# Stores moved to GpSimd, sums of x on engines, and an earlier first fetch in a fused attention and two-MLP kernel

## The chip, the cores and the metric

The kernel runs on one core of a Trainium2 chip. The metric is the device time of one execution in microseconds (us); of several timed runs the median counts. The profile is of one further execution.

## The reference

Sliding-window attention with sink columns feeds two MLPs in a row, all in float32.

```python
# q, k, v: [2, 8, 768, 64]; window 128, 4 sink columns
a = softmax(where(is_sink | in_window, q @ k.T / 8, -1e9))
x = (a @ v).transpose(0, 2, 1, 3).reshape(1536, 512)
# first MLP: 512 -> 2048 -> 512
h = x @ w_in
g = where(h >= 1, h, where(h <= -1, 0, (h + 1) ** 2 / 4))
x = g @ w_out
# second MLP, its own weights
h = x @ w_in
out = (h * clip(h + 3, 0, 6) / 6) @ w_out
```

The weights come in as float64.

## The kernel before

x is held transposed, [512, 1536], as 4 blocks of 128 rows (KC) and 3 chunks of 512 tokens (NCH). The 2048 features are 16 chunks of 128 (FC), taken in 8 pairs. For float32 accuracy every operand of TensorE is split into a high and a low part; a product is three matmuls (high x high, high x low, low x high) for each 128 rows.

**Weights.** `load_w` fetches a pair of one weight (1 MB, 64-bit words) into one of two raw buffers; `narrow` turns the words into float32 with integer operations on VectorE and ScalarE, `split` makes the parts (`high` on either engine, `low` on VectorE). w_out's parts are also stored to DRAM (`wo_d`), since they are used twice. `turn_weights` does this for the next pair and asks for a further load three ticks later; `issued` and `taken` count both. From the third pair on (PLAIN is 2), `combine` also makes four sums of blocks of w_in, for a form of block multiplication that needs fewer products (`paired`, with the matching sums of x from `combine_x`). The sums are made in the raw buffer.

**Two stages for each MLP (m is 0 or 1).** First stage: for each chunk of features, h for the three token chunks. Token chunk 0 goes on at once: `activate`, then `y_group` accumulates its output in four PSUM banks. Token chunks 1 and 2 are kept in one of four buffers (`hq`) and stored to DRAM (`spill` to `h_d`). In `paired` a part of them is added in DRAM by an accumulating DMA (`add_c`). Second stage: `fetch` brings h back, `activate` and `y_group` run for chunks 1 and 2, and `load_wo` brings the split w_out back, into one of three buffers.

**Order.** TensorE's and SyncE's instructions keep the order of the program; the other engines' order is chosen by a scheduler with a timeline of its own, and is then fixed. Each queue runs in order. All DMAs but the accumulating ones are issued by SyncE (SP). `tick` and `defer` place work some groups later in the program.

In the code: the end of the first stage, its fetches and loads, and `start` are at the end of the main loop; L627 is the matmul of `product`, L779 that of `y_group`; L137 and L144 are `high` and `low`; L603 to L608 are `activate`; L677 is the subtraction in `combine_x`, L673 and L674 its DMAs; L715 and L710 evict products in `paired`; L719 is `add_c`; L189 to L199 are `narrow`; L642 is `spill`, L648 `fetch`, L276 `load_wo`, L233 the store of w_out's parts.

Of the kernel before, what the change touches and what calls it, by code (L numbers as in the profile page):

```python
# [71 lines left out]
def sink_attention_moe_moe_kernel(  # L72
# [75 lines left out]
    def x_tiles(m, c):  # L148
        if (m, c) not in xparts:
            xparts[m, c] = tuple(  # L150
                x_p.tile([P, KC, N], F32R, tag=f"x{part}{c}", name=f"x{part}{m}_{c}") for part in "hl"
            )
        return xparts[m, c]
# [47 lines left out]
    def take(m, which, p, half=None):  # L201

        fs = slice(0, 2) if half is None else slice(half, half + 1)
        n = DM * (fs.stop - fs.start)
        last = half is None or half == 1
        if (m, which, p) not in wtile:
            if which == "i":
                w = wi_p.tile([P, 2, 2, DM], F32R, tag="wi", name=f"wi{m}")
                for e in range(2):
                    wi[m, 2 * p + e] = tuple(w[:, x, e, :].rearrange("p (k f) -> p k f", f=P) for x in range(2))  # L210
            else:
                w = wo_tile(m, p)
            t = raw[m, which, p]
            if wide:
                t32 = raw_p.tile([P, 2, DM], F32, tag=f"w{which}32", name="w32", bufs=2 if which == "i" else 1)
            else:
                t32 = t
            wtile[m, which, p] = (w, t, t32)
        w, t, t32 = wtile[m, which, p]
        if last:  # L220
            raw.pop((m, which, p))
            wtile.pop((m, which, p))
        if which == "i":
            hi, lo = w[:, 0, fs, :], w[:, 1, fs, :]
        else:
            hi, lo = w[:, fs, 0, :], w[:, fs, 1, :]

        def split():
            high(hi, t32[:, fs], n)
            defer(lambda: low(lo, t32[:, fs], hi, n))  # L230
            if last and which == "o":
                defer(
                    lambda: nc.sync.dma_start(out=wo_d[m][p], in_=f32(w.rearrange("p t a f -> p (t a f)"))), 4  # L233
                )
            if last and which == "i" and p >= PLAIN:
                defer(lambda: combine(m, p, t, t32))
# [9 lines left out]
    def combine(m, p, t, t32):  # L246
# [47 lines left out]
    def build_fast_attention(at_p):  # L294
# [178 lines left out]
        def mix(j):  # L473
# [30 lines left out]
            xh, xl = x_tiles(0, GROUPS[gi][0])  # L504
            cs = slice(col0[gi], col0[gi] + n)
            high(xh[:, hp, cs], ps, n, True)
            low(xl[:, hp, cs], ps, xh[:, hp, cs], n)
# [79 lines left out]
    def load_x1():  # L587
        for c in range(NCH):
            xh, xl = x_tiles(0, c)
            for kc in range(KC):  # L590
                t = g_p.tile([P, N], F32, tag="r", name="xraw")
                nc.sync.dma_start(out=t, in_=x1_d[0][kc * P:(kc + 1) * P, c * N:(c + 1) * N])
                high(xh[:, kc, :], t, N)
                low(xl[:, kc, :], t, xh[:, kc, :], N)

    def activate(m, fc, c, h, g, psum):

        r = g_p.tile([P, N], F32, tag="r", name="r")
        gh = g_p.tile([P, N], F32R, tag="gh", name="gh", bufs=3)
        gl = g_p.tile([P, N], F32R, tag="gl", name="gl", bufs=3)  # L600
        with tc.high_priority(200):
            if m == 0:
                nc.scalar.activation(out=r, in_=h, func=AF.Relu, scale=0.5, bias=half)  # L603
                nc.scalar.activation(out=r, in_=r, func=AF.Square)  # L604
                nc.vector.scalar_tensor_tensor(out=g, in0=r, scalar=1.0, in1=h, op0=ALU.min, op1=ALU.max)
# [3 lines left out]
        bal.add("act", (2 - m) * (260 + N / 1.2))  # L609
        bal.add("dve", 150 + N / 0.96)  # L610
# [12 lines left out]
    def product(ps, w, x, start=True):  # L623
        (hi, lo), (xh, xl) = w, x
        ops = [(a, b, kc) for kc in range(hi.shape[1]) for a, b in ((hi, xh), (hi, xl), (lo, xh))]
        for i, (a, b, kc) in enumerate(ops):
            nc.tensor.matmul(  # L627
                ps, a[:, kc, :], b[:, kc, :], start=start and i == 0, stop=i == len(ops) - 1,
# [21 lines left out]
    def h_group(m, fc, c):  # L650
        ps = bank_h()
        product(ps, wi[m, fc], x_tiles(m, c))
        if c == 0:
            activate(m, fc, c, ps, ps, True)
# [6 lines left out]
    xt = {}  # L661

    def combine_x(m):

        t = st_p[0].tile([P, 2, 4, HK, N], F32R, tag="xt", name=f"xt{m}", bufs=1)
        xt[m] = [tuple(t[:, x, i] for x in range(2)) for i in range(4)]
# [3 lines left out]
        for i, (c, k) in enumerate(blocks):  # L670
            xh, xl = x_tiles(m, c)
            ks = slice(k * HK, (k + 1) * HK)
            nc.sync.dma_start(out=u[i], in_=f32(xh[:, ks, :]))  # L673
            nc.gpsimd.dma_start(out=u[i], in_=f32(xl[:, ks, :]), accum_op=ALU.add)  # L674
# [18 lines left out]
    def paired(m, p):  # L693
# [11 lines left out]
        def part(x, ks):  # L705
            return tuple(v[:, ks, :] for v in x)
# [18 lines left out]
        product(a, part(wi[m, f0], k0), part(xb, k0))  # L725
# [4 lines left out]
        product(a, part(wi[m, f0], k1), part(xb, k1), start=False)  # L730
        put(hf0[:, 0], a)
        tick()
# [18 lines left out]
        plus(hf1[:, 0], b)  # L751
        tick()
        product(c, s4, part(xc, k1), start=False)
# [5 lines left out]
    def y_group(m, fc, c):  # L759
# [11 lines left out]
        if last:  # L771
            if m == 0:
                xh, xl = x_tiles(1, c)
            else:
                o = x_p.tile([P, KC, N], F32, tag=f"xh{c}", name=f"o{c}")
        for dm in range(KC):
# [4 lines left out]
            if last:  # L781
                with tc.high_priority(400):
                    if m == 0:
                        high(xh[:, dm, :], ys[dm], N, True)
                        low(xl[:, dm, :], ys[dm], xh[:, dm, :], N)
                    elif dm % 2 == 0:
                        nc.scalar.activation(out=o[:, dm, :], in_=ys[dm], func=AF.Copy)
# [24 lines left out]
    with tc.manual_schedule(engines={mybir.EngineType.PE, mybir.EngineType.SP}):  # L812
        nc.vector.memset(half, 0.5)
        make_identity(nc, ident)
        if fast:
            with tc.tile_pool(name="at", bufs=2) as at_p:
                build_fast_attention(at_p)
                halves = {112: ("i", 0), 100: ("i", 1), 88: ("o", 0), 76: ("o", 1)}
                for n, step in enumerate(steps):
# [27 lines left out]
        issued[0] = taken[0] = 2  # L847
        st_p.append(ctx.enter_context(tc.tile_pool(name="st", bufs=2)))

        for m in range(2):  # L850
            for p in range(NP):
# [3 lines left out]
                for fc in (2 * p, 2 * p + 1):  # L855
# [27 lines left out]
            order = [(m, fc, c) for fc in range(FC) for c in (1, 2)]  # L883

            def start(k):
                _, fc, c = order[k]
                t = held[m, fc][:, c - 1]
                activate(m, fc, c, t, t, False)

            start(0)  # L890
            start(1)
            y_group(m, FC - 1, 0)
            tick()
            for n, (_, fc, c) in enumerate(order):
# [4 lines left out]
                if n + 2 < len(order):  # L899
                    start(n + 2)  # L900
# [50 lines left out]
```

## Time and profile before

| | |
|---|---|
| median of 3 runs | 689.57 us (688.48 to 691.66) |
| the profiled execution | 683.08 us, span 681.3 us |
| mean granted clock of TensorE | 0.970 |
| TensorE matmuls (PE) | 620.5 us busy, 91% of the span, 2,880 instructions |
| weight loads (PEld) | 482.6 us, 71% |
| VectorE (DVE) | 437.7 us, 64% |
| ScalarE (ACT) | 368.9 us, 54% |
| GpSimd (POOL) | 87.0 us, 13%, nearly all in the attention stage |
| DMA | 129.6 MB, 190 GB/s on average |

Attention lies in the first 111 us, the first stages at 111 to 289 and 395 to 572, the second ones at 298 to 395 and 582 to 677. Busy shares are averages over stages that wait for different things, and matmuls overlap in the pipeline with modelled ends, so that the number of matmuls in a stretch says more than the busy time.

### The profile page before, as it was taken

How to read it: one execution, taken by the hardware profiler on the slowest of the kernel's cores; microseconds unless marked ns; L12 is line 12 of the kernel's file. 1: busy time of each engine (PE TensorE's matmuls, PEld its weight loads, DVE VectorE, ACT ScalarE, POOL GpSimd, SP SyncE). 2: the span in 40 equal slices, each digit the busy share in tenths (PEclk: the TensorE clock that was granted, in tenths of full speed). 3: DMA queues.
4: the chain of work that ended last, by engine and by line, in shares of the span. 5: the costliest groups of instructions: out<-in, count | busy, mean ns of one | idle time of the engine just before them, and what ended most of it. 6: DMA issues, size and time to landing. Idle time of an engine off the chain costs nothing.

```text
span 681.3 us, 8173 instructions
## 1 busy us (share of the span) xinstructions
PE 620.5 (91%) x2880; PEld 482.6 (71%) x2880; DVE 437.7 (64%) x835; ACT 368.9 (54%) x671; POOL 87.0 (13%) x112
## 2 busy tenths in 40 slices
PE   7999899979999998959999997999999996899897
PEld 4666566858777776748767785888778884787676
DVE  5778886399787887344433846888877614545553
ACT  6878776377565656376564736465654514431211
POOL 6766751100000000000000020000000000000000
PEclk9999898979999999969999998999999998899999
DMA  6456213956687775485435587466687535944423
GB/s 209 131 159 190 61 63 134 285 200 246 248 254 241 214 242 166 106 291 211 158 124 199 203 248 220 160 229 207 208 250 235 189 93 176 342 166 157 167 105 125
DMA packets 42297, 129.60 MB, mean 190 GB/s; under 512 B 3600, under 2 KB 13328, under 8 KB 38160
## 3 DMA queue, kind: packets, MB, share of 16 engines
q1 hardware_dynamic: 37840, 118.58, 49.2%
q0 software_dynamic: 4416, 10.49, 9.2%
q8 instruction: 23, 0.38, 0.2%
q14 instruction: 18, 0.15, 0.1%
HBM read 77.68 MB, written 42.99 MB: 177 GB/s over the span
## 4 chain that ended last, share of the span: by engine, by line
DMA 32%; PE 30%; DVE 22%; ACT 11%; issue 3%; SPq 1%; POOL 0%; ACTq 0%; DVEq 0%; POOLq 0%
PE ps_y L779 13%; DMA hq<-h_d 12%; PE ps_h L627 11%; DMA raw0i<-moe_w_in_dram 5%; DMA raw1i<-moe_w_in_dram 3%; ACT p L425 3%; DVE w L194 3%; DVE w L199 3%; DVE gl L144 3%; DMA raw0o<-moe_w_out_dram 3%; ACT r L603 2%; DMA raw1o<-moe_w_out_dram 2%; DMA x<-xl 2%; DMA h_d<-hq 2%; ACT w L189 2%
## 5 line engine op out<-in xcount | busy, mean ns | idle before, releaser
L779 PE MATMUL ps_y<-gh,wo 128*128 128x512 f32 x768 | 251.1, 399 | 22.3 <-DMA wo<-wo_d 18.1
L779 PEld LDWEIGHTS ps_y<-gh,wo 128*128 128x128 f32 x768 | 148.1, 193 | 58.4 <-ACT r L604 9.4
L779 PE MATMUL ps_y<-gl,wo 128*128 128x512 f32 x384 | 154.9, 403 | 12.7 <-DVE gl L144 12.7
L627 PE MATMUL ps_h<-xh,wi 128*128 128x512 f32 x480 | 156.2, 391 | 2.0 <-ACT p L710 1.9
L627 PEld LDWEIGHTS ps_h<-xh,wi 128*128 128x128 f32 x480 | 90.5, 189 | 22.8 <-ACT p L710 3.1
L779 PEld LDWEIGHTS ps_y<-gl,wo 128*128 128x128 f32 x384 | 74.1, 193 | 33.7 <-DVE gl L144 18.7
L627 PE MATMUL ps_h<-xl,wi 128*128 128x512 f32 x240 | 93.7, 390 | 0.0
L144 DVE TENSOR_TENSOR gl<-hq,gh 128x512 fp32r<-128x512 f32 x64 | 44.0, 688 | 48.5 <-ACT gh L137 47.7
L416 POOL TENSOR_SCALAR p<-p,sm 128x260 f32<-128x260 f32 (+2 forms) x72 | 62.6, 885 | 34.0 <-DVE psk L407 18.7
L192 DVE TENSOR_SCALAR w<-w 128x1024 f32<-128x1024 f32 (+1 forms) x34 | 22.7, 668 | 58.2 <-ACT w L189 58.0
L425 ACT ACTIVATE p<-p,nm 128x260 f32<-128x260 f32 (+2 forms) x96 | 46.2, 483 | 16.2 <-DVE nm L392 16.0
L719 POOL DMA_DIRECT2D h_d<-ct x12 | 13.0, 1086 | 323.5 <-DMA h_d<-hq 76.6
L627 PE MATMUL ps_h<-xt,st 128*128 128x512 f32 x216 | 53.2, 390 | 0.7 <-DVE hq L715 0.7
L627 PEld LDWEIGHTS ps_h<-xl,wi 128*128 128x128 f32 x240 | 45.2, 188 | 9.2
L607 ACT ACTIVATE r<-hq,half 128x512 f32<-128x512 f32 x32 | 21.6, 715 | 49.1 <-DMA hq<-h_d 48.8
L627 PEld LDWEIGHTS ps_h<-xt,st 128*128 128x128 f32 x216 | 40.5, 188 | 9.5 <-DVE hq L715 1.1
L608 DVE SCALAR_TENSOR_TENSOR hq<-r,hq 128x512 f32<-128x512 f32 x32 | 21.5, 689 | 34.5 <-ACT r L607 34.5
L603 ACT ACTIVATE r<-hq,half 128x512 f32<-128x512 f32 x32 | 21.5, 714 | 35.6 <-DMA hq<-h_d 35.6
L392 DVE CUSTOM_DVE_ANT_0 p<-ps_s,mask 128x260 f32<-128x260 f32 (+2 forms) x96 | 34.4, 396 | 6.5 <-POOL mask L311 3.8
L379 PE MATMUL ps_s<-kraw,qraw 64*128 64x260 f32 (+2 forms) x192 | 32.4, 431 | 6.1 <-DMA kraw<-k_dram 4.4
L715 DVE TENSOR_TENSOR hq<-ps_h,p 128x512 f32<-128x512 f32 x36 | 24.6, 684 | 18.1 <-PE ps_h L627 18.1
L137 ACT ACTIVATE gh<-hq 128x512 fp32r<-128x512 f32 x43 | 26.5, 620 | 10.1 <-PE ps_y L779 9.4
(104 smaller groups left out, 862.7 us busy)
## 6 DMA issues: line engine op xcount, KB each, us to landing
h_d<-hq SPq DMA_DIRECT2D x32, 512.0 KB, 4.5
wo_d<-wo SPq DMA_DIRECT2D x16, 1024.0 KB, 9.3
hq<-h_d SPq DMA_DIRECT2D x32, 512.0 KB, 4.3
wo<-wo_d SPq DMA_DIRECT2D x16, 1024.0 KB, 6.8
raw1i<-moe_w_in_dram SPq DMA_DIRECT2D x8, 1024.0 KB, 7.0
raw1o<-moe_w_out_dram SPq DMA_DIRECT2D x8, 1024.0 KB, 9.1
raw0i<-moe_w_in_dram SPq DMA_DIRECT2D x7, 1024.0 KB, 6.1
raw0o<-moe_w_out_dram SPq DMA_DIRECT2D x7, 1024.0 KB, 9.9
```

The lines of the kernel that those rows point to most:

```text
L137: nc.scalar.activation(out=dst, in_=src, func=AF.Copy)
L144: nc.vector.tensor_tensor(out=dst, in0=src, in1=f32(hi), op=ALU.subtract)
L192: nc.vector.tensor_scalar(out=f32(c), in0=f32(c), scalar1=F64_LOW, scalar2=F64_HIGH, op0=ALU.max, op1=ALU.min)
L379: nc.tensor.matmul(banks[e], tq[rows, u * P:(u + 1) * P], tk[rows, c0:c0 + w], start=True, stop=True)
L392: nc.vector.tensor_tensor_reduce(out=p[:, e, :], in0=banks[e], in1=masks[min(i, 2)], scale=-SCALE, scalar=BIG, op0=ALU.add, op1=ALU.min, a ...
L416: nc.gpsimd.tensor_scalar_mul(out=px, in0=px, scalar1=r)
L425: nc.scalar.activation(out=p[:, e, :], in_=p[:, e, :], func=AF.Exp, scale=-1.0, bias=nm[:, v + e:v + e + 1], accum_out=sm[:, v + e:v + e + 1],
L603: nc.scalar.activation(out=r, in_=h, func=AF.Relu, scale=0.5, bias=half)
L607: nc.scalar.activation(out=r, in_=h, func=AF.Relu, scale=1.0 / 6.0, bias=half)
L627: nc.tensor.matmul(ps, a[:, kc, :], b[:, kc, :], start=start and i == 0, stop=i == len(ops) - 1, skip_group_check=not start,)
L715: nc.vector.tensor_tensor(out=dst, in0=src, in1=p1, op=ALU.add)
L779: nc.tensor.matmul(ys[dm], a[:, cs], b, start=fc == 0 and i == 0, stop=last and i == 2)
```

## The change

Stores of h and of w_out's parts are issued by GpSimd. The sums of weights are made in scratch tiles that share memory with parts of x (x is now allocated in halves of two blocks, so that a half can be given up). The sums of x are made by VectorE and GpSimd instead of DMAs. In the last pair the first two fetches of h and loads of w_out, and the first two activations, are issued. The activation of fetched h leaves its result in r, which has three buffers; for the first MLP its Square becomes a VectorE operation.

```diff
-    def x_tiles(m, c):
+    def x_half(m, c, part, k):
...
+            xparts[m, c, part, k] = x_p.tile([P, HK, N], F32R, tag=f"x{part}{c}{k}", name=f"x{part}{m}_{c}{k}")
...
-                    lambda: nc.sync.dma_start(out=wo_d[m][p], in_=f32(w.rearrange("p t a f -> p (t a f)"))), 4
+                    lambda: nc.gpsimd.dma_start(out=wo_d[m][p], in_=f32(w.rearrange("p t a f -> p (t a f)"))), 4
...
-                t[:, fs].rearrange("p t f w -> p (t f) w"), t32[:, fs].rearrange("p t f -> p (t f)"), m == 0 and p == 0
+                t[:, fs].rearrange("p t f w -> p (t f) w"), t32[:, fs].rearrange("p t f -> p (t f)"), m == 0 and p < PLAIN
...
-        if wide:
-            s = f32(t.rearrange("p t f w -> p (t f w)"))[:, 0:4 * hw].rearrange("p (s f) -> p s f", f=hw)
+        if p == PLAIN:
+            s = st_p[0].tile([P, 4, hw], F32, tag="ct", name="s32", bufs=1)
         else:
-            s = raw_p.tile([P, 4, hw], F32, tag="s32", name="s32", bufs=1)
+            s = x_p.tile([P, 4, hw], F32, tag="xh20", name="s32")
...
-    def activate(m, fc, c, h, g, psum):
-
-        r = g_p.tile([P, N], F32, tag="r", name="r")
+    def activate(m, fc, c, h, psum):
+
+        r = g_p.tile([P, N], F32, tag="r", name="r", bufs=3)
...
+        g = h if psum else r
...
                 nc.scalar.activation(out=r, in_=h, func=AF.Relu, scale=0.5, bias=half)
-                nc.scalar.activation(out=r, in_=r, func=AF.Square)
-                nc.vector.scalar_tensor_tensor(out=g, in0=r, scalar=1.0, in1=h, op0=ALU.min, op1=ALU.max)
+                if psum:
+                    nc.scalar.activation(out=r, in_=r, func=AF.Square)
+                    nc.vector.scalar_tensor_tensor(out=g, in0=r, scalar=1.0, in1=h, op0=ALU.min, op1=ALU.max)
+                else:
+                    nc.vector.scalar_tensor_tensor(out=r, in0=r, scalar=1.0, in1=r, op0=ALU.min, op1=ALU.mult)
+                    nc.vector.tensor_tensor(out=g, in0=h, in1=r, op=ALU.max)
...
     def spill(m, fc):
...
-        nc.sync.dma_start(out=h_d[m][fc // 2][:, e:e + 2, :], in_=t)
+        nc.gpsimd.dma_start(out=h_d[m][fc // 2][:, e:e + 2, :], in_=t)
...
+    order = [(fc, c) for fc in range(FC) for c in (1, 2)]
+
+    def start(m, k):
+        fc, c = order[k]
+        t = held[m, fc][:, c - 1]
+        activate(m, fc, c, t, False)
...
-            nc.sync.dma_start(out=u[i], in_=f32(xh[:, ks, :]))
-            nc.gpsimd.dma_start(out=u[i], in_=f32(xl[:, ks, :]), accum_op=ALU.add)
+            xh, xl = (x_half(m, c, part, k) for part in "hl")
+            (nc.vector if i % 2 else nc.gpsimd).tensor_tensor(out=u[i], in0=f32(xh), in1=f32(xl), op=ALU.add)
...
     def paired(m, p):
...
-        p1 = st_p[0].tile([P, N], F32, tag="p1", name="p1")
-        ct = st_p[0].tile([P, 2, N], F32, tag="ct", name="ct", bufs=1)
+        p1 = st_p[0].tile([P, N], F32, tag="p1", name="p1", bufs=1)
+        if p % 2:
+            ct = x_p.tile([P, 2, N], F32, tag="xl20", name="ct")
+        else:
+            ct = st_p[0].tile([P, 2, N], F32, tag="ct", name="ct", bufs=1)
...
         put(hf0[:, 0], a)
+        if last:
+            fetch(m, 0)
+            load_wo(m, 0)
+            fetch(m, 1)
+            load_wo(m, 1)
         tick()
...
         plus(hf1[:, 0], b)
-        tick()
-        product(c, s4, part(xc, k1), start=False)
+        if last:
+            start(m, 0)
+            start(m, 1)
+        tick()
+        product(c, s4, x_tiles(m, 2, k1), start=False)
...
+                    if left == 3:
+                        load_w(0, "i", 1)
...
-        issued[0] = taken[0] = 2
+        issued[0] = 3 if fast else 2
+        taken[0] = 2
...
-                            load_weights()
-                        if (m, p) == (0, 0):
-                            defer(load_weights, 3)
+                            if issued[0] == 2:
+                                load_weights()
...
+            y_group(m, FC - 1, 0)
             flush()
-            for fc in range(3):
-                fetch(m, fc)
-            for p in range(WO - 1):
-                load_wo(m, p)
...
-            start(0)
-            start(1)
-            y_group(m, FC - 1, 0)
-            tick()
+            fetch(m, 2)
```

## Rows read from the trace of the kernel before

**Rows 1.** Timeline of PE: start, duration, engine, line, matmuls, count, [idle before <- releaser].
```profile
277.57 2.88 PE L627 MATMUL ps_h<-xt,st 128*128 128x512 f32 x12
...
297.66 0.77 PE L779 MATMUL ps_y<-gh,wo 128*128 128x512 f32 x1 [9.05 <-DMA wo<-wo_d]
```

**Rows 2.** Stretches of the span: length, busy us (x instructions) of each engine.
```profile
core 0: us, PE busy (x) PEld busy (x) DVE busy (x) ACT busy (x) POOL busy (x), PEclk, DMA share, GB/s
136.00:153.00 17.00, 12.63 (x44) 9.65 (x44) 17.00 (x20) 13.37 (x18) 0.00 (x0) 0.80 0.54 203
153.00:272.00 119.00, 112.27 (x486) 90.32 (x485) 96.89 (x128) 74.25 (x98) 5.43 (x5) 1.00 0.72 230
...
289.00:306.00 17.00, 8.34 (x27) 6.70 (x28) 8.16 (x14) 12.04 (x22) 1.08 (x1) 0.70 0.85 296
306.00:391.00 85.00, 81.18 (x339) 62.60 (x338) 42.63 (x64) 49.81 (x83) 0.00 (x0) 1.00 0.49 180
...
374.00:391.00 17.00, 16.29 (x71) 12.93 (x70) 15.00 (x19) 12.92 (x18) 0.00 (x0) 1.00 0.54 221
...
408.00:442.00 34.00, 28.98 (x116) 23.41 (x115) 24.95 (x30) 18.48 (x23) 0.00 (x0) 0.90 0.59 187
442.00:561.00 119.00, 117.15 (x513) 95.81 (x512) 83.60 (x113) 61.20 (x80) 5.43 (x5) 1.00 0.64 202
561.00:595.00 34.00, 24.96 (x102) 20.23 (x101) 14.99 (x24) 14.98 (x25) 1.08 (x1) 0.85 0.75 260
595.00:663.00 68.00, 64.22 (x273) 50.58 (x272) 34.72 (x62) 15.95 (x25) 0.00 (x0) 1.00 0.44 154
```

**Rows 3.** Timeline of SP's queue where layer 0's stages meet.
```profile
285.70 1.72 SPq L648 DMA_DIRECT2D hq<-h_d  x3
287.51 1.06 SPq L276 DMA_DIRECT2D wo<-wo_d  x2
```

**Rows 4.** The chain that ended last, one turn of it in the second stage: start, us.
```profile
343.69 3.97 DMA hq<-h_d
347.75 1.34 ACT r L603 x2
349.64 0.70 DVE gl L144
```

**Rows 5.** The same chain where x is summed, in layer 0 and in layer 1.
```profile
116.38 17.02 DMA raw0i<-moe_w_in_dram
...
405.25 13.13 DMA x<-xl
```

**Rows 6.** Timeline of PE: two waits in the first stages.
```profile
262.48 1.65 PE L627 MATMUL ps_h<-xt,wi 128*128 128x512 f32 x6 [2.63 <-DVE hq L715]
...
422.63 0.80 PE L779 MATMUL ps_y<-gl,wo 128*128 128x512 f32 x1 [5.01 <-DVE gl L144]
```

**Rows 7.** Timeline of VectorE: a wait for weights, and the last parts of x.
```profile
257.54 0.69 DVE L192 TENSOR_SCALAR w<-w 128x1024 f32<-128x1024 f32 x1 [4.54 <-ACT w L189]
...
392.65 4.87 DVE L144 TENSOR_TENSOR xl<-ps_y,xh 128x512 fp32r<-128x512 f32 x8
```

**Rows 8.** DMA issues: queue, count, KB each, median us to landing.
```profile
hq<-h_d SPq DMA_DIRECT2D x32, 512.0 KB, 4.3
...
raw0o<-moe_w_out_dram SPq DMA_DIRECT2D x7, 1024.0 KB, 9.9
h_d<-ct POOLq DMA_DIRECT2D x12, 512.0 KB, 6.7
...
x<-xl POOLq DMA_DIRECT2D x8, 512.0 KB, 13.7
```

**Rows 9.** Line 719: duration ns min/median/max, first and last start.
```profile
L719 POOL DMA_DIRECT2D h_d<-ct x12: 1082/1084/1097, 188.4 to 573.0; - x12
```

**Rows 10.** Groups by line and shape: busy us, mean ns, idle before.
```profile
L416 POOL TENSOR_SCALAR p<-p,sm 128x260 f32<-128x260 f32 x48 | 45.7, 968 | 27.2 <-DVE psk L407 18.7 <-ACT p L425 5.2 <-ACT pts L443 2.3
...
L677 DVE TENSOR_TENSOR x<-x 128x1024 f32<-128x1024 f32 x4 | 4.9, 1217 | 0.0
```

More of the change, by code (lines that the diff above doesn't have):

```diff
@@ L146, in sink_attention_moe_moe_kernel, with x_at, x_tiles @@
     xparts = {}
-    def x_tiles(m, c):
[L149 to L153, printed above, removed]
+    def x_half(m, c, part, k):
+        if (m, c, part, k) not in xparts:
+            xparts[m, c, part, k] = x_p.tile([P, HK, N], F32R, tag=f"x{part}{c}{k}", name=f"x{part}{m}_{c}{k}")
+        return xparts[m, c, part, k]
+    def x_at(m, c, part, kc):
+        return x_half(m, c, part, kc // HK)[:, kc % HK, :]
+    def x_tiles(m, c, kcs=None):
+        return tuple([x_at(m, c, part, kc) for kc in (kcs or range(KC))] for part in "hl")
     half = consts.tile([P, 1], F32, name="half")
@@ L503, in mix @@
             n = nq * P
-            xh, xl = x_tiles(0, GROUPS[gi][0])
             cs = slice(col0[gi], col0[gi] + n)
-            high(xh[:, hp, cs], ps, n, True)
-            low(xl[:, hp, cs], ps, xh[:, hp, cs], n)
+            xh, xl = (x_at(0, GROUPS[gi][0], part, hp)[:, cs] for part in "hl")
+            high(xh, ps, n, True)
+            low(xl, ps, xh, n)
         units = [(j, u) for j in range(len(pairs)) for u in range(geom(pairs[j][0])[2])]
@@ L627, in product @@
             nc.tensor.matmul(
-                ps, a[:, kc, :], b[:, kc, :], start=start and i == 0, stop=i == len(ops) - 1,
+                ps, a[:, kc, :], b[kc], start=start and i == 0, stop=i == len(ops) - 1,
                 skip_group_check=not start,
@@ L653, in h_group @@
         if c == 0:
-            activate(m, fc, c, ps, ps, True)
+            activate(m, fc, c, ps, True)
         else:
@@ L724, in paired @@
         a = bank_h()
-        product(a, part(wi[m, f0], k0), part(xb, k0))
+        product(a, part(wi[m, f0], k0), x_tiles(m, 1, k0))
         put(p1, a)
@@ L729, in paired @@
         tick()
-        product(a, part(wi[m, f0], k1), part(xb, k1), start=False)
+        product(a, part(wi[m, f0], k1), x_tiles(m, 1, k1), start=False)
         put(hf0[:, 0], a)
+        if last:
[3 more added lines that the diff above has]
+            load_wo(m, 1)
         tick()
@@ L770, in y_group @@
         last = fc == FC - 1
[L771 to L775, printed above, removed]
+        if last and m == 0:
+            xh, xl = x_tiles(1, c)
         for dm in range(KC):
@@ L783, in y_group @@
                     if m == 0:
[L784 to L787, printed above, removed]
-                    else:
-                        nc.vector.tensor_copy(out=o[:, dm, :], in_=ys[dm])
+                        high(xh[dm], ys[dm], N, True)
+                        low(xl[dm], ys[dm], xh[dm], N)
+                    else:
+                        if dm % HK == 0:
+                            o = x_p.tile([P, HK, N], F32, tag=f"xh{c}{dm // HK}", name=f"o{c}")
+                        if dm % 2 == 0:
+                            nc.scalar.activation(out=o[:, dm % HK, :], in_=ys[dm], func=AF.Copy)
+                        else:
+                            nc.vector.tensor_copy(out=o[:, dm % HK, :], in_=ys[dm])
                 if m:
-                    nc.sync.dma_start(out=out[cs, c * N:(c + 1) * N], in_=o[:, dm, :])
+                    nc.sync.dma_start(out=out[cs, c * N:(c + 1) * N], in_=o[:, dm % HK, :])
     queue = [(m, which, p) for m in range(2) for p in range(NP) for which in "io"]
@@ L877, in sink_attention_moe_moe_kernel @@
                     tick()
+            y_group(m, FC - 1, 0)
             flush()
-            for fc in range(3):
-                fetch(m, fc)
-            for p in range(WO - 1):
-                load_wo(m, p)
[L883 to L888, printed above, removed]
-            start(0)
-            start(1)
-            y_group(m, FC - 1, 0)
-            tick()
-            for n, (_, fc, c) in enumerate(order):
+            fetch(m, 2)
+            for n, (fc, c) in enumerate(order):
                 if c == 1:
```

28 lines of the change are left out of this document (13 added, 15 removed).

## The prediction

> **What bounds the kernel now.** I read the stretch table first, then TensorE's gaps in the timeline, then the chain of waits through those gaps. TensorE runs 2,880 matmuls and no other engine is as busy, so the yardstick is its pitch: a run of twelve 128x512 matmuls takes 2.88 us, of which 0.39 is the tail of the last, so one goes in every 0.2265 us, and 17 us hold 75 of them [rows 1]. Against that the table shows what each stretch lost: a stretch of T us should hold T/0.2265 matmuls, and each missing one is 0.2265 us [rows 2].
>
> - 136 to 153: 44 of 75, 7.0 us lost. 153 to 272 (the paired stage of layer 0): 486 of 525, 8.8 us.
> - 289 to 306 (between the two stages of layer 0): 27 of 75, 10.9 us. 306 to 391 (second stage): 339 of 375, 8.2 us.
> - 408 to 442: 116 of 150, 7.7 us. 442 to 561: 513 of 525, 2.7 us.
> - 561 to 595 (between the stages of layer 1): 102 of 150, 10.9 us. 595 to 663: 273 of 300, 6.1 us.
>
> Together 62 us: the most that this change can give back, since the attention stage before 111 us and the number of matmuls stay as they are. What each loss waits for:
> - Between the stages TensorE stands 9.05 us for wo, twice, and then goes at the lower clock (0.70 mean in that stretch) [rows 1, 2]. The loads of h and wo are issued only at 285.70 and 287.51, behind the last store of h, the wo ones behind three fetches of h [rows 3].
> - In the second stage the chain is a loop: fetch of h 3.97 us, Relu, then the low part of an older group on VectorE, which frees the buffer for the next fetch [rows 4]. From 343.69 to 350.34 it turns once, 6.65 us, while two groups of twelve matmuls need 5.44.
> - At 116 to 133 a weight load takes 17.02 us beside the DMAs that sum x, and the VectorE work that it holds back then fills 136 to 153 completely (17.00 of 17) [rows 2, 5]. In layer 1 the summing DMA takes 13.13 us, a subtraction in VectorE's queue waits for it, the next low part stands behind, and TensorE waits 5.01 us [rows 5, 6].
> - In the paired stage VectorE waits for a weight load (4.54 us), and TensorE for VectorE's eviction (2.63 us) [rows 6, 7].
>
> **The change part by part.**
> *Fetch in the last pair.* fetch(0), load_wo(0), fetch(1), load_wo(1) move into the last pair, 54 matmuls or 12.2 us earlier in the order, and the first two activations before its last product. Their buffers are free: h buffers 0 and 1 belong to the pair before, of three wo buffers one is two pairs old and the second is freed by the y group emitted just ahead. SP in that place has nothing else left to wait for. So both gaps go, with the low clock behind them: 21.8 us at most. Late next are fetch(2) and fetch(3). The store of chunk 15 leaves just before 285.70, 1.1 us to issue on POOL, 6.7 to land, 4.3 to fetch back: 297.8 [rows 3, 8, 9]. It is wanted by group 6, at 288.6 + 6 x 2.72 = 304.9 less 3.4 us of activation: 301.5. Slack 3.7 us; if the store landed as slowly as the summing DMAs of x (13.7 median) it would be 3.3 us late. In layer 1 fetch(2) stands behind four output stores and has about no slack. I take 20.5, bounds 14 and 21.8.
>
> *Activation with its result in r, three buffers.* h is now free after the first VectorE operations instead of after the low part, and an activation can be only three groups ahead. The fetch of chunk k+4 then goes out when chunk k has been activated and is wanted when its own turn comes, eight groups or 21.8 us later, against 4.3 us to land [rows 8]: the loop goes, 14.3 us at most. The Square moves from ACT to VectorE as a second operation like its others of 0.70 us: three or 2.1 us in a group of 2.72 us [rows 4]. That is hidden, except where layer 0 ends: at 374 to 391 VectorE already has 15.00 of 17 us because weights are turned there, and 6 x 0.70 = 4.2 us more don't fit by 2.2 [rows 2]. I take 11.5, bounds 5 and 14.3.
>
> *Sums of x on engines.* Eight loads and eight accumulating loads go; four adds on VectorE of 1.22 us each and four on POOL come. No row shows a two-input POOL operation. The nearest, 128x260 with one input, takes 0.968 us: by length 3.8 us for 128x1024, by two inputs 7.6; from below VectorE's own 1.22 [rows 10]. I take 3.8. In layer 1 the last parts of x are written at 397.5 [rows 7]; two POOL adds end at 405.1 (399.9 to 412.7), 13 us ahead of the DMA's 418.4 [rows 5], so even the upper end takes away the wait. In layer 0 they take the place of DMAs that run beside the slow weight load. The Trainium skill (GPSIMD Engine Reference, Performance versus the Vector engine) gives 4,497 ns for 2,048 elements, by which it would be an estimated 2.25 us; the sum is unchanged.
>
> *Stores on POOL, weights' sums in a scratch of their own.* In the first stage SP holds nothing but weight loads now. The program asks for them one turn later, but SP meets no store and no x load, so a load goes as soon as a raw buffer is free; and for w_in that is now after the narrowing, not after the low part of the sums. The load that took 17.02 us loses its company and is issued some 3 us earlier. So I give back 5 of the 7.0 us at 136 (four extra VectorE adds stay), 6 of 7.7 at 408, 5 of 8.8 and 0.7 of 2.7 in the paired stages, where VectorE keeps 96.89 us of work in 119 [rows 2], 88% once these are shorter, and some waits for it stay. Bounds: 0 and all of it, 26.2.
>
> The price: per pair POOL issues two stores of h, one of wo and the accumulation, 4 x 1.08 = 4.3 us, and waits for the landing of a store before accumulating, for which I take the accumulation's own 6.7 us (up to 13.7 as for x): 11 to 18 of 20.4 us (90 matmuls) [rows 8, 9]. Its engine has nothing else then. h buffers turn over in two pairs, so a late store is covered by some 40 us. I take 3.5 us for stores that land later and for POOL and VectorE in each other's way; bounds 0 and 20 (below). Sharing the x tiles in halves, p1 with one buffer and ct with two places cost nothing that I can find: p1's last reader is three groups ahead of its next writer.
>
> One rule speaks against the stores. The twelve DMAs that POOL issues take 1,082 to 1,097 ns each, whatever VectorE does beside them [rows 9]. The Trainium skill (SBUF — State Buffer, SBUF: two separate sides) says that a VectorE operation in a two-port mode locks POOL out, so that descriptors wait. By that rule each store is late by a VectorE operation, and only the last one of a layer has a reader close behind it; the sum would be the same within 1.4 us.
>
> *Sum:* 20.5 + 11.5 + 16.7 - 3.5 = 45.2. The profiled execution took 683.1 us (span 681.3, 1.8 us around it that stay), so about 638 there; the median of the timed runs is 6.5 us above it, and I take the same 45 off that: 645 us.
>
> **Rivals.**
> *POOL and VectorE exclude each other in the first stage.* If VectorE stood for the 4.3 us of each pair's POOL issues, its load of 0.81 x 20.4 = 16.6 us would be 20.9 of 20.4: no gain is left in the first stage, and 0.5 to 1.5 us more a pair, 12 pairs. For: VectorE's share [rows 2]. Against: POOL's issues of before keep one length [rows 9]. Gain 32 less 6 to 18: 664 to 676.
> *The early fetch isn't early.* If the fetches in the last pair are held (a buffer, or SP behind a weight load), the two gaps stay: 645 + 20.5 = 665. Against: weights have all been asked for by then.
> *VectorE becomes the bound of the second stage.* Its queue has a fixed order, and a Relu that waits for a fetch, or the second operation, stands ahead of a low part: 0.3 us a group over 64 groups is 19 us: 664. Against: 42.63 of 85 us busy now [rows 2].
> *Slower: weights come too late.* The program asks for each weight load one turn later than before. If that, and not the raw buffer, sets its issue, a load has one h group (2.7 us) until it is turned, and one of w_out lands after 9.9 us (median) [rows 8]. VectorE then stands 7.2 us at each of 14 such turns; the 19% that it has free, 3.8 us a pair, hides a part, and 3.4 x 14 = 47 us stay. Less the gains of 32 that don't hang on it: 705 us. It decides from 2.3 us unhidden a turn (32/14); the row where VectorE waits 4.54 us for a load shows that such waits reach TensorE [rows 6, 7]. Against: nothing else waits in SP's queue.
>
> **How the numbers follow.** Forecast 0.65 (632 to 660 by the ends of its own terms that I hold likely), POOL against VectorE 0.11, late fetch 0.08, second stage on VectorE 0.10, weights late 0.06. Range 632 to 672: at its low end 58 of the 62 us come back (689.6 - 58), its high end takes in the late fetch, VectorE's bound and half of the first rival. A measurement of this kernel can tell about 0.5% from no change. Faster by more than that: 0.91 (all but late weights and two rivals at once), within 0.03, slower 0.06.
>
> **What would show it.** Right: no wait for wo at the ends of the first stages, and the granted clock 1.0 there (2.4 GHz); second stages of 87 us for 32 groups; no VectorE wait on an x sum; weight loads issued without a store ahead. Wrong: Relu waiting for h fetches again; VectorE full through the pairs; POOL's stores queued until h buffers run out; TensorE waiting for the first groups of a second stage.

## The result and the profile after

The median went from 689.03 us (684.76 to 691.66, 4 runs) to 637.10 us (635.62 to 639.48, 4 runs): a ratio of 0.9255, 95% interval 0.9198 to 0.9312. That is 7.9 us below the forecast of 645 and inside its range. The profiled execution took 639.48 us, the slowest of its four, with a span of 637.6 us and a granted clock of 0.981; the one before took 683.08 us (span 681.3, clock 0.970), a little under all four of its timed runs. So the two traces lie 43.7 us of span apart and the medians 51.9. The working below goes by the traces; the other 8 us are in no trace that I have. Runs more than 1.5% above the fastest of their kernel are left out of every ratio.

Stretches of the kernel after, columns as in [rows 2]:

```profile
113.80:130.00 16.20, 9.56 (x28) 7.33 (x29) 16.16 (x15) 5.94 (x8) 4.68 (x4) 0.68 0.61 213
130.00:281.50 151.50, 150.15 (x661) 123.70 (x660) 119.63 (x160) 96.06 (x129) 18.71 (x26) 1.00 0.69 224
281.50:372.60 91.10, 89.68 (x395) 73.74 (x394) 74.84 (x110) 53.24 (x77) 2.19 (x3) 1.00 0.62 214
372.60:394.10 21.50, 16.75 (x65) 12.55 (x64) 21.50 (x28) 11.25 (x17) 5.95 (x4) 0.92 0.47 172
394.10:543.80 149.70, 149.70 (x662) 123.93 (x661) 103.07 (x136) 76.50 (x102) 17.27 (x25) 1.00 0.61 193
543.80:633.60 89.80, 89.75 (x396) 74.02 (x395) 45.16 (x69) 39.72 (x60) 1.64 (x2) 1.00 0.54 189
```

By the same yardstick (0.2265 us a matmul) they lose 9.9 (28 of 71.5), 1.8 (661 of 669), 1.6 (395 of 402), 6.8 (65 of 95), 0 and 0 us. Two losses are left, both where new x meets the first weights of a layer, and VectorE is busy through both, 16.16 of 16.20 and 21.50 of 21.50 us. Four of the six stretches run at TensorE's pitch, or within 2% of it, at a clock of 1.00.

The joint between the stages is gone. In SP's queue the first fetch and the first load of wo go out while the first stage still runs ([rows 3] had them at 285.70 and 287.51), and the chain of waits (start, us, what) shows the second stages as unbroken runs of y groups, where [rows 4] had a loop:

```profile
254.55 0.34 SPq L657 DMA_DIRECT2D hq<-h_d  x1
255.00 0.37 SPq L280 DMA_DIRECT2D wo<-wo_d  x1
```
```profile
281.54 65.29 PE ps_y L800 x288
...
543.80 89.77 PE ps_y L800 x396
```

What stands in the two losses that are left. Timeline of VectorE, then of POOL, then of TensorE (the bracket is the idle time before, and its releaser):

```profile
111.47 0.69 DVE L196 TENSOR_SCALAR w<-w 128x1024 f32<-128x1024 f32 x1 [0.18 <-ACT w L193]
112.08 2.89 DVE L197 TENSOR_SCALAR raw0i<-raw0i 128x1024 int32<-128x1024 int32 x1
114.89 2.82 DVE L203 CUSTOM_DVE_ANT_0 w<-raw0o,w 128x1024 uint16<-128x1024 uint16 x1
117.63 0.68 DVE L139 CAST xh<-ps_v 128x512 fp32r<-128x512 f32 x1
...
374.52 3.04 DVE L203 CUSTOM_DVE_ANT_0 w<-raw1i,w 128x2048 uint16<-128x2048 uint16 x1
...
378.62 3.07 DVE L144 TENSOR_TENSOR xl<-ps_y,xh 128x512 fp32r<-128x512 f32 x5
```
```profile
111.75 5.41 POOL L687 TENSOR_TENSOR x<-xh,xl 128x1024 f32<-128x1024 f32 x2 [8.41 <-ACT w L193]
...
374.08 2.39 POOL L687 TENSOR_TENSOR x<-xh,xl 128x1024 f32<-128x1024 f32 x1 [13.57 <-DVE xl L144]
...
379.58 2.42 POOL L687 TENSOR_TENSOR x<-xh,xl 128x1024 f32<-128x1024 f32 x1
```
```profile
118.36 0.79 PE L636 MATMUL ps_h<-xh,wi 128*128 128x512 f32 x1 [4.56 <-DVE xh L139]
...
121.23 0.80 PE L636 MATMUL ps_h<-xl,wi 128*128 128x512 f32 x1 [2.08 <-DVE xl L144]
...
390.03 0.79 PE L800 MATMUL ps_y<-gl,wo 128*128 128x512 f32 x1 [3.92 <-DVE gl L144]
```

POOL's two adds end at 117.16. Beside them one masking operation takes 2.89 us instead of 0.69 (L196, of the same shape, is just ahead of it), and one narrowing add 2.82 us, though its median at twice the length is 1.22; each of the two ends shortly after an add has ended. The cast that TensorE waits for stands behind them. At 374.52 it is the same, 3.04 us instead of 1.22. The five low parts at 378.62, which read PSUM, keep their 0.6 us each although a POOL add starts at 379.58. The Trainium skill (SBUF — State Buffer, SBUF: two separate sides) says that VectorE and GpSimd share a pair of ports under an exclusive lock: a VectorE operation in a two-port mode, or with two inputs in SBUF (this one only against a GpSimd operation that reads SBUF), and a GpSimd operation hold each other off for a whole instruction. The trace agrees, with the 2.2 us extra of 2.89 for 0.69.

The stores on POOL, one line each (duration ns min/median/max, first and last start), and their landings (KB each, median us):

```profile
L651 POOL DMA_DIRECT2D h_d<-hq x32: 531/533/1128, 123.4 to 543.9; - x32
```
```profile
L237 POOL DMA_DIRECT2D wo_d<-wo x16: 531/546/777, 122.1 to 492.1; - x16
```
```profile
L687 POOL TENSOR_TENSOR x<-xh,xl x4: 2394/2537/2782, 111.8 to 379.6; 128x1024 f32<-128x1024 f32 x4
```
```profile
wo_d<-wo POOLq DMA_DIRECT2D x16, 1024.0 KB, 5.0
h_d<-hq POOLq DMA_DIRECT2D x32, 512.0 KB, 3.9
```

### The profile page after: what moved, and what is told of

Same layout as the page of the kernel before. It is cut to its first block, busy times and chain, and to the rows that moved or that the text cites. A ratio compares the mean times of both kernels' runs of the same rounds, so it can differ in the third digit from the quotient of the medians.

```text
span 637.6 us, 8180 instructions
## 1 busy us (share of the span) xinstructions
PE 608.0 (95%) x2880; PEld 482.5 (76%) x2880; DVE 465.7 (73%) x855; ACT 366.7 (58%) x655; POOL 118.9 (19%) x156
## 4 chain that ended last, share of the span: by engine, by line
PE 66%; DVE 12%; ACT 10%; DMA 7%; issue 3%; POOL 0%; SPq 0%; DVEq 0%; ACTq 0%; POOLq 0%
PE ps_y L800 34%; PE ps_h L636 27%; ACT p L429 4%; DMA raw0i<-moe_w_in_dram 3%; DMA raw1i<-moe_w_in_dram 2%; PE ps_v L503 2%; DVE w L203 2%; DMA raw0o<-moe_w_out_dram 2%; ACT w L193 2%; PE ps_s L383 1%; DVE p L396 1%; DVE w L198 1%; DVE xl L144 1%; ACT raw0o L201 1%; PE ps_v L487 1%
## 5 line engine op out<-in xcount | busy, mean ns | idle before, releaser
L800 PE MATMUL ps_y<-gh,wo 128*128 128x512 f32 x768 | 243.1, 391 | 0.3 <-ACT gh L137 0.2
L800 PEld LDWEIGHTS ps_y<-gh,wo 128*128 128x128 f32 x768 | 144.9, 189 | 31.1 <-ACT gh L137 1.1
L636 PE MATMUL ps_h<-xh,wi 128*128 128x512 f32 x480 | 158.7, 397 | 5.8 <-DVE xh L139 4.6
L800 PE MATMUL ps_y<-gl,wo 128*128 128x512 f32 x384 | 150.4, 392 | 5.2 <-DVE gl L144 5.2
L144 DVE TENSOR_TENSOR gl<-r,gh 128x512 fp32r<-128x512 f32 x64 | 44.1, 690 | 16.6 <-ACT gh L137 16.3
L651 POOL DMA_DIRECT2D h_d<-hq x32 | 19.4, 607 | 192.3 <-DVE hq L731 100.0
L137 ACT ACTIVATE gh<-r 128x512 fp32r<-128x512 f32 x59 | 37.1, 629 | 27.6 <-PE ps_y L800 26.3
L617 DVE SCALAR_TENSOR_TENSOR r<-r,hq 128x512 f32<-128x512 f32 x32 | 21.9, 692 | 23.2 <-ACT r L616 23.2
L616 ACT ACTIVATE r<-hq,half 128x512 f32<-128x512 f32 x32 | 22.9, 723 | 25.3 <-DVE gl L144 21.2
L608 ACT ACTIVATE r<-hq,half 128x512 f32<-128x512 f32 x32 | 23.0, 722 | 20.7 <-DVE gl L144 19.6
L237 POOL DMA_DIRECT2D wo_d<-wo x16 | 9.0, 560 | 132.5 <-DVE wo L144 132.5
```

The costliest lines, as they stand in the source:

```text
L137: nc.scalar.activation(out=dst, in_=src, func=AF.Copy)
L144: nc.vector.tensor_tensor(out=dst, in0=src, in1=f32(hi), op=ALU.subtract)
L616: nc.scalar.activation(out=r, in_=h, func=AF.Relu, scale=1.0 / 6.0, bias=half)
L636: nc.tensor.matmul(ps, a[:, kc, :], b[kc], start=start and i == 0, stop=i == len(ops) - 1, skip_group_check=not start,)
L800: nc.tensor.matmul(ys[dm], a[:, cs], b, start=fc == 0 and i == 0, stop=last and i == 2)
```

## The experiments

The theory: (a) the joints come back through the earlier fetch, (b) the loop through the Relu with its result in r, (c) the paired stages through raw buffers that are free sooner, (d) the two losses that are left come from POOL's adds locking VectorE. Rivals: (a') the joints come back because the stores left SP's queue; (c') it is the DMA sums of x that went; (d') VectorE simply has too much to do there, whoever adds. Code is shown cut, "..." marks what is left out. Each kernel is the changed one with one edit, unless the text says otherwise. A number behind "ratio" is to the kernel before, with its interval.

**e1_late_fetch**: the fetches, loads and first activations where they were before.
```diff
-        if last:
-            fetch(m, 0)
-            load_wo(m, 0)
-            fetch(m, 1)
-            load_wo(m, 1)
...
-        if last:
-            start(m, 0)
-            start(m, 1)
...
+            for fc in range(3):
+                fetch(m, fc)
+            for p in range(WO - 1):
+                load_wo(m, p)
+            start(m, 0)
+            start(m, 1)
             y_group(m, FC - 1, 0)
```


> The changed kernel, with the first fetches, loads of wo and activations put back behind the last pair. My theory: TensorE stands some 9 us for wo at the end of each first stage again and goes at the lower clock behind it, 637 + 21.8 = about 658 us. Rival (with the stores off SP's queue and three r buffers the place of the fetch hardly matters): the two waits shrink to 2 or 3 us each, about 643 us.


Measured: 638.83 us, ratio 0.9308 (0.924 to 0.9377), not to be told from the changed kernel. My theory (a) fell. SP's queue shows why: with no store in it SP is far ahead of the program, and issues the "late" fetches at 249 to 270, before the stage ends.
```profile
249.43 20.72 SPq L657 DMA_DIRECT2D hq<-h_d  x3
270.26 0.84 SPq L280 DMA_DIRECT2D wo<-wo_d  x2
```

**e3_sp_stores**: both kinds of stores back on SP, the fetch stays early.
```diff
-        nc.gpsimd.dma_start(out=h_d[m][fc // 2][:, e:e + 2, :], in_=t)
+        nc.sync.dma_start(out=h_d[m][fc // 2][:, e:e + 2, :], in_=t)
```
(and the same for `wo_d`)


> The changed kernel, with the stores of h and of w_out's parts issued by SP again. My theory: the weight loads stand behind stores again and the paired stages lose again what they gained, 9.7 us: about 647 us. Rival (the paired stages gained by the raw buffers that are free earlier, the queue is no matter): 637 to 640 us. By the rule that POOL's stores starve it would be faster, under 634 us.


Measured: 634.73 us, ratio 0.9248 (0.9178 to 0.9317), the same. My theory fell. Stores on SP land in much the same time as on POOL (3.9 and 5.0 above), and the joints stay closed:
```profile
h_d<-hq SPq DMA_DIRECT2D x32, 512.0 KB, 3.3
wo_d<-wo SPq DMA_DIRECT2D x16, 1024.0 KB, 5.1
```
The weights do come later. VectorE's first operation on converted weights shows it (the last figures are VectorE's idle time just ahead of it, and what ended most of that): 58.2 us in the kernel before, 34.8 in e3, and 9.7 in the changed kernel. Even so the paired stages of e3 lose only 1.8 us (657 of 665 matmuls at 127 to 277.6) and 0.1 us (644 of 645 at 391 to 537). First the kernel before, then e3:
```profile
L192 DVE TENSOR_SCALAR w<-w 128x1024 f32<-128x1024 f32 (+1 forms) x34 | 22.7, 668 | 58.2 <-ACT w L189 58.0
```
```profile
L196 DVE TENSOR_SCALAR w<-w 128x1024 f32<-128x1024 f32 (+1 forms) x34 | 22.8, 670 | 34.8 <-ACT w L193 34.8
```

**e9_late_and_sp**: both edits together, since either alone left the gain.
```diff
-            fetch(m, 0)
-            load_wo(m, 0)
-            fetch(m, 1)
-            load_wo(m, 1)
...
-        nc.gpsimd.dma_start(out=h_d[m][fc // 2][:, e:e + 2, :], in_=t)
+        nc.sync.dma_start(out=h_d[m][fc // 2][:, e:e + 2, :], in_=t)
```


> The changed kernel, with the first fetches behind the last pair and the stores on SP. Each alone cost nothing (638.8 and 634.7 us). Theory (either is enough to bring wo in time: an early place in the queue, or a queue that doesn't stand at stores): together they bring the two waits of some 9 us back, with the low clock behind them: 655 to 660 us. Rival (the waits went for another reason, such as the activations or the scheduler's order): 633 to 641 us.


Measured: 658.39 us, ratio 0.9584 (0.9523 to 0.9646): 21 us slower than the changed kernel. SP stands among the h stores for 18.85 us, the fetches follow, and TensorE waits 9.54 us for wo (in layer 1 9.72), as in [rows 1, 3]. First SP's queue, then TensorE:
```profile
261.04 18.85 SPq L651 DMA_DIRECT2D h_d<-hq  x3
279.98 1.71 SPq L657 DMA_DIRECT2D hq<-h_d  x3
281.79 1.17 SPq L280 DMA_DIRECT2D wo<-wo_d  x2
```
```profile
292.43 0.77 PE L792 MATMUL ps_y<-gh,wo 128*128 128x512 f32 x1 [9.54 <-DMA wo<-wo_d]
```

**e7_early_fetch_alone**: the kernel before, with nothing but the early fetch.
```diff
+        if last:
+            fetch(m, 0)
+            load_wo(m, 0)
+            fetch(m, 1)
+            load_wo(m, 1)
         tick()
...
+        if last:
+            start(m, 0)
+            start(m, 1)
         tick()
```


> The kernel before, with only the first fetches, loads of wo and activations moved into the last pair. Theory (the place alone takes away the two waits for wo, whoever issues the stores): 689 - 20 = about 669 us. Rival (SP stands at stores of h in the last pair and the fetches are late there too): 680 to 689 us.


Measured: 668.33 us, ratio 0.9741 (0.9654 to 0.9828), 19 us less than the kernel before beside it (687.33), with no wait for wo left in the trace. So the joints are worth some 20 us, and the early place and the empty SP queue are two keys to one door.

**e2_in_place**: the activation of fetched h in place again, with the Square on ScalarE and two r buffers.
```diff
-        r = g_p.tile([P, N], F32, tag="r", name="r", bufs=3)
+        r = g_p.tile([P, N], F32, tag="r", name="r", bufs=2)
...
-        g = h if psum else r
+        g = h
...
-                    nc.vector.scalar_tensor_tensor(out=r, in0=r, scalar=1.0, in1=r, op0=ALU.min, op1=ALU.mult)
-                    nc.vector.tensor_tensor(out=g, in0=h, in1=r, op=ALU.max)
+                nc.scalar.activation(out=r, in_=r, func=AF.Square)
+                nc.vector.scalar_tensor_tensor(out=g, in0=r, scalar=1.0, in1=h, op0=ALU.min, op1=ALU.max)
```


> The changed kernel, with the activation of fetched h in place again (result in the h buffer, Square on ScalarE, two r buffers). My theory: the loop of fetch, Relu and low part is back and the second stages lose some 12.7 us again, about 650 us. Rival (the loop came from the late start of the second stage, when all four buffers were empty at once): about 640 us.


Measured: 657.30 us, ratio 0.9563 (0.951 to 0.9616): 20 us slower, where I had said 12.7. The second stages take 100.3 and 102.0 us and lose 10.8 and 9.8 us; the chain is the loop of [rows 4] again, 6.84 us from one fetch to the next, where two groups need 5.44. Stretches, then the chain:
```profile
276.50:376.80 100.30, 94.25 (x395) 72.89 (x393) 52.05 (x78) 61.92 (x105) 1.80 (x3) 1.00 0.56 194
549.00:651.00 102.00, 96.55 (x407) 76.52 (x405) 50.29 (x87) 28.17 (x45) 1.64 (x2) 0.98 0.49 167
```
```profile
303.78 4.14 DMA hq<-h_d
...
308.01 1.34 ACT r L608 x2
...
309.90 0.70 DVE gl L144
...
310.62 4.44 DMA hq<-h_d
```
So (b) holds for the activation as a whole. Its three parts (the result's place, the Square's engine, the third r buffer) were undone together; that the place is what matters is read from the chain, where the fetch waits for the low part that frees h.

**e6_sums_in_raw**: the sums of weights made in the raw buffer again.
```diff
-        if p == PLAIN:
-            s = st_p[0].tile([P, 4, hw], F32, tag="ct", name="s32", bufs=1)
-        else:
-            s = x_p.tile([P, 4, hw], F32, tag="xh20", name="s32")
+        s = f32(t.rearrange("p t f w -> p (t f w)"))[:, 0:4 * hw].rearrange("p (s f) -> p s f", f=hw)
```


> The changed kernel, with the four sums of w_in's blocks made in the raw buffer again, which is then free later. Theory (this is what shortened the paired stages, since putting the stores back on SP lost nothing): TensorE waits for VectorE's evictions again in layer 0, 642 to 647 us. Rival (SP's freedom from x loads, or the scheduler's other order, did it): 635 to 639 us.


Measured: 650.23 us, ratio 0.9463 (0.9402 to 0.9523), 13 us slower. The waits of [rows 6, 7] are back: VectorE waits for the conversion of late weights, and TensorE 4.07 us (then 2.96 and 2.48) for an eviction behind it. VectorE, then TensorE:
```profile
231.11 0.69 DVE L196 TENSOR_SCALAR w<-w 128x1024 f32<-128x1024 f32 x1 [3.91 <-ACT w L193]
...
236.76 0.69 DVE L196 TENSOR_SCALAR w<-w 128x1024 f32<-128x1024 f32 x1 [1.73 <-ACT w L193]
...
237.97 0.68 DVE L728 TENSOR_TENSOR hq<-ps_h,p 128x512 f32<-128x512 f32 x1
```
```profile
238.71 2.08 PE L633 MATMUL ps_h<-xt,wi 128*128 128x512 f32 x6 [4.07 <-DVE hq L728]
```
So (c) holds. It is not the sum of VectorE's waits for weights that costs: that is 33.2 us here and 34.8 in e3, which loses hardly anything in the paired stages. Here two of these waits stand ahead of an eviction that TensorE needs.

**e5_x_dma**: the sums of x by DMA again.
```diff
-            (nc.vector if i % 2 else nc.gpsimd).tensor_tensor(out=u[i], in0=f32(xh), in1=f32(xl), op=ALU.add)
+            nc.sync.dma_start(out=u[i], in_=f32(xh))
+            nc.gpsimd.dma_start(out=u[i], in_=f32(xl), accum_op=ALU.add)
```


> The changed kernel, with the sums of x made by DMAs as before (a load and an accumulating load for each). The engines' sums leave waits of 6.6 us at 114 to 121 in layer 0 and 3.9 us at 386 in layer 1, about as long as the DMAs' did. Theory (the sums were worth nothing: one wait was changed for another): 635 to 641 us. Rival (the DMA sums would now also hold up the weight loads behind them on SP, so that the sums on engines were worth some 10 us): 645 to 650 us.


Measured: 638.75 us, ratio 0.9309 (0.9239 to 0.9379), the same as with sums on engines. Without the lock TensorE still waits 1.23 us at 112, 1.22 and 2.19 us at 138 to 142, 3.36 us at 392 and 2.54 us at 410, and the paired stages lose no more than 2.6 us each. (c') is out: this part of the change was worth nothing that can be measured.

**e4_x_dve**: all four sums of a layer on VectorE.
```diff
-            (nc.vector if i % 2 else nc.gpsimd).tensor_tensor(out=u[i], in0=f32(xh), in1=f32(xl), op=ALU.add)
+            nc.vector.tensor_tensor(out=u[i], in0=f32(xh), in1=f32(xl), op=ALU.add)
```


> The changed kernel, with all four sums of x of a layer on VectorE, none on POOL. My theory: a POOL sum of 2.4 to 2.8 us holds up a VectorE operation that runs beside it (2.89 us in place of 0.69), so VectorE gains more than the two adds of 1.2 us cost it: TensorE's wait of 4.56 us for the last part of x in layer 0 shrinks below 1.5 us, and the time falls by 3 to 8 us, to about 632. Rival (POOL takes load off a full VectorE, the long operations are a matter of the profile): 638 to 642 us.


Measured: 636.05 us, ratio 0.9260 (0.9205 to 0.9315). The lock is gone, 0.69 us for both operations, and the wait for the cast is 0.20 us; but the adds stand ahead of the low part, and TensorE waits 4.63 us there. VectorE, then TensorE:
```profile
108.83 0.69 DVE L197 TENSOR_SCALAR raw0i<-raw0i 128x1024 int32<-128x1024 int32 x1
109.43 0.69 DVE L203 CUSTOM_DVE_ANT_0 w<-raw0o,w 128x1024 uint16<-128x1024 uint16 x1
110.03 0.68 DVE L139 CAST xh<-ps_v 128x512 fp32r<-128x512 f32 x1
110.63 3.48 DVE L687 TENSOR_TENSOR x<-xh,xl 128x1024 f32<-128x1024 f32 x3
```
```profile
115.91 0.80 PE L636 MATMUL ps_h<-xl,wi 128*128 128x512 f32 x1 [4.63 <-DVE xl L144]
```
The lock is shown as a mechanism. Taking it away, with the adds on VectorE here or in DMAs in e5, gave nothing in the total, but put other work in its place. So (d') was put to four orders of the same work.

**e8_x_dve_in_order**: as e4, and the adds keep the program's place, behind the low parts.
```diff
-            (nc.vector if i % 2 else nc.gpsimd).tensor_tensor(out=u[i], in0=f32(xh), in1=f32(xl), op=ALU.add)
+            tc.keep_in_program_order(nc.vector.tensor_tensor(out=u[i], in0=f32(xh), in1=f32(xl), op=ALU.add))
+            bal.add("dve", 150 + HK * N / 0.96)
```
The last line books the add in the program's own count of VectorE's load, by which it chooses engines for other operations; e4 has no such line.


> The changed kernel, with all sums of x on VectorE and these adds kept in the order of the program, so that they stand behind the low part of x that TensorE waits for (with the adds on VectorE alone the wait moved from the high part, 0.2 us, to the low part, 4.6 us). Theory (order, not the amount of VectorE work, made that wait): it falls below 1.5 us, and the time to 630 to 634 us. Rival (VectorE is full there and the wait turns up a few groups later): 636 to 640 us.


Measured: 640.81 us, ratio 0.9364 (0.931 to 0.9417). The wait for the low part falls to 1.23 us, and three others come by 146, 1.40, 1.87 and, on weights, 2.38 us:
```profile
130.41 0.50 PE L801 MATMUL ps_y<-gl,wo 128*128 128x512 f32 x1 [1.87 <-DVE gl L144]
...
145.35 0.80 PE L801 MATMUL ps_y<-gh,wo 128*128 128x512 f32 x1 [2.38 <-ACT wo L137]
```

**e10_in_order_both**: as e8, and the narrowing of layer 1's first weights is pinned to the program's order too.
```diff
-                t[:, fs].rearrange("p t f w -> p (t f) w"), t32[:, fs].rearrange("p t f -> p (t f)"), m == 0 and p < PLAIN
+                t[:, fs].rearrange("p t f w -> p (t f) w"), t32[:, fs].rearrange("p t f -> p (t f)"), p < PLAIN or (m == 1 and p == PLAIN)
```


> As the kernel before it in this list, and the narrowing of layer 1's first three weights of either kind also kept in program order. Theory (in layer 1 VectorE is full at 373 to 394 because weights that nobody needs yet are narrowed early): the wait of 3.9 us for a low part goes, 627 to 632 us. Rival (kept in order, they come late for their own products): 636 to 645 us.


Measured: 637.60 us, ratio 0.9282 (0.9228 to 0.9335). The start of layer 1 is clean, 134 matmuls where the changed kernel has 102 in the same 30 us (first e10, then the changed kernel). In the paired stages TensorE waits for evictions, 1.10, 1.16 and 1.90 us in layer 0 and 1.87 us in layer 1. Only the last can be what VectorE has put off in layer 1; e8 has the 1.90 us too. Layer 0's start keeps e8's waits. Below the two stretches is the 1.90:
```profile
366.00:396.00 30.00, 30.00 (x134) 24.83 (x133) 26.36 (x33) 17.02 (x25) 1.09 (x2) 1.00 0.35 131
```
```profile
366.00:396.00 30.00, 25.25 (x102) 19.57 (x101) 29.85 (x37) 17.21 (x24) 5.95 (x4) 0.94 0.38 139
```
```profile
223.38 1.66 PE L636 MATMUL ps_h<-xt,wi 128*128 128x512 f32 x6 [1.90 <-DVE hq L732]
```

**e11_in_order_sp** (e8 with the stores on SP) and **e12_x_dve_narrow_in_order** (e4 with e10's second edit). Beside e8's and e4's own edits they have:
```diff
-        nc.gpsimd.dma_start(out=h_d[m][fc // 2][:, e:e + 2, :], in_=t)
+        nc.sync.dma_start(out=h_d[m][fc // 2][:, e:e + 2, :], in_=t)
```
```diff
-                t[:, fs].rearrange("p t f w -> p (t f) w"), t32[:, fs].rearrange("p t f -> p (t f)"), m == 0 and p < PLAIN
+                t[:, fs].rearrange("p t f w -> p (t f) w"), t32[:, fs].rearrange("p t f -> p (t f)"), p < PLAIN or (m == 1 and p == PLAIN)
```


> As the first of this list, with the stores of h and of w_out's parts on SP. On SP they hold back the weight loads a little and cost nothing (634.7 us, and no wait at layer 1's start). Theory (POOL isn't needed for the stores): 626 to 632 us, the same as the first or some us below. Rival (with SP blocked by stores the early fetches have no spare time): 640 us or more.

> The changed kernel, with all sums of x on VectorE (not kept in order) and layer 1's first three narrowings of either kind kept in program order: the two versions that had the shortest waits at the start of layer 0 and of layer 1. Theory (the waits add up, 5 us in layer 0 as with the adds on VectorE, none in layer 1): 629 to 634 us, ratio 0.918 to 0.925 of the kernel before. Rival (VectorE has the same work in either order, and the wait turns up elsewhere): 635 to 641 us.


Measured: 642.18 us, ratio 0.9296 (0.9229 to 0.9363), and 641.28 us, ratio 0.9351 (0.9324 to 0.9377), the second with waits of 4.64 us in layer 0 and of 1.63, 1.61 and 2.60 us at 391 to 439.

None of the four orders came into the range of its theory and none beats the changed kernel, and three edits to who adds or when (e4, e8, e5) stay within 4 us. But (d') does not hold as it stands either. In the 30 us in which the changed kernel issues 102 matmuls, e3 has VectorE just as full (29.90 us against 29.85) and POOL's two adds beside it, and issues 134, as many as fit:
```profile
366.00:396.00 30.00, 30.00 (x134) 24.81 (x133) 29.90 (x37) 19.47 (x28) 5.76 (x2) 1.00 0.27 97
```
So at layer 1's start neither a full VectorE nor the adds on POOL cost TensorE anything by themselves. What is left is the order in VectorE's queue: what stands ahead of the operation that TensorE waits for. That is argued, not shown. Layer 0's waits stay in e3, 4.56 and 2.26 us. Its profiled span is 7.0 us shorter than the changed kernel's, but the ratios of the two (0.9248 and 0.9255) can't be told apart.

## Why the prediction was right, and where it was not

By its own terms, lost us before against after, from the two tables of stretches:

| term | forecast to come back | came back |
|---|---|---|
| joints between the stages | 20.5 of 21.8 | 21.8 |
| loop in the second stages | 11.5 of 14.3 | 12.7 |
| start of layer 0 | 5 of 7.0 | -2.9 (9.9 lost) |
| start of layer 1 | 6 of 7.7 | 0.9 (6.8 lost) |
| paired stages | 5.7 of 11.5 | 9.7 |
| price of the stores | -3.5 | 0 (e3) |
| sum | 45.2 | 42.2, of 43.7 in the spans |

That the sum came within 3 us of the forecast is partly luck: the two starts fell short by 13.0 us together, and the four other terms came in 10.0 us above.

- *Joints.* The size was right, the reason half so. I gave the gain to the 12.2 us by which the fetch moves up. e1 and e3 show that the place isn't needed once SP holds no stores, nor the empty queue once the place is early; e9 needs both undone to lose 21 us. The forecast had the deciding fact in a half-sentence ("SP in that place has nothing else left to wait for") and didn't ask what that alone would do. Its rival "the early fetch isn't early" did not occur: both remedies would have had to fail.
- *Loop.* Right, and mis-sized from below. The stretches of [rows 2] held 51 groups (612 matmuls) that lost 14.3 us, 0.28 us a group; e2's two stages hold 67 groups (802 matmuls) that lose 20.6 us, 0.31 a group. In the kernel before, the first groups of each stage stood in the joint's wait, which gave their fetches a head start. So the two gains overlap: undone alone, the loop costs 20 us and not 14. e7 agrees: with the joints closed and the loop left, its second stages lose 7.6 us (385 matmuls at 283.2 to 378) and 10.2 us (363 at 562.6 to 655). VectorE did not become the bound there: it has 74.84 of 91.1 us in layer 0's second stage, and 1.6 us are lost.
- *Sums of x.* This step failed. For POOL's add I took 3.8 us between 1.22 and 7.6; it is 2.54 us in the median. (The estimate of 2.25 us by the Trainium skill, GPSIMD Engine Reference, Performance versus the Vector engine, was the nearer one; the four adds took 2.39 to 2.78.) The size was not the fault. I counted the adds as work beside the path, and the DMA's wait as a gain. But new x, sums and first weights come due on VectorE together, and what was a wait for a DMA became a queue on VectorE, in this kernel's order longer by the lock: 4.56 and 2.08 us at 114 to 121, 3.92 us at 386 to 390, with the clock at 0.68 in the first of these stretches. With DMA sums in the new kernel (e5) the total is the same. The rival "POOL and VectorE exclude each other" named the right pair in the wrong place: the adds do, the 48 plain issues have medians of 533 and 546 ns.
- *Stores and scratch.* Right in direction, too small for the paired stages. They lose 1.8 us where I left 5.8, and e6 shows that the scratch is the cause, worth 13 us. The emptier SP queue, which I counted beside it, is worth nothing there that can be measured: with the stores (e3) or the x loads (e5) back in it the total is the same, though VectorE then stands 34.8 and 30.9 us for converted weights. Late weights, the forecast's slower rival, did not come.
- *Price of the stores.* I charged 1.08 us an issue by the accumulating DMAs' row [rows 9]; a plain one costs half, and e3 shows no price in the total. Six of the 48 took longer, 0.78 to 1.13 us.

What stays open: whether the 9.9 and 6.8 us at the starts of the layers can be had in the total. Layer 1's start is clean in the traces of e3 and e10, and layer 0's in none; five orders (e4, e8, e10, e11, e12) moved the waits about and the time stayed.

## What to carry to other kernels

When two parts of a change could each open the same wait, undo them singly and together: single undoing calls both worthless here, and together they are worth 21 us. A wait that vanishes is a gain only if the work that replaces it does not stand ahead of something that is waited for. An engine that is busy through a whole stretch (16.16 of 16.20 us) is a warning that its share of the span (73%) hides, but no proof: 29.90 of 30 us cost nothing in e3. Read its queue there, operation by operation. A loop's price read from the kernel before is a lower bound where another stall hides some of its turns.

## What the runs showed of the hardware

- A GpSimd add of two 128x1024 tiles holds up VectorE operations between SBUF tiles until it ends (0.69 became 2.89 us, 1.22 became 3.04; e1 and e9 have 2.89 and 3.06, 2.88 and 3.05), while VectorE operations that read PSUM ran beside it at 0.6 us each.
- A plain DMA issue on GpSimd took 0.53 us, an accumulating one 1.10 us (L735, median 1,100 ns). Stores issued by GpSimd landed about as fast as those by SP: 3.9 against 3.3 us for 512 KB, 5.0 against 5.1 us for 1 MB.
